# A zeroing memset in front of one row-tile load of a transformer block

## The chip, the cores and the metric

The kernel runs on one core of one Trainium2 chip. The metric is the device time of one execution in microseconds (us), as the median of several runs. The engines are named as the profile names them: PE is TensorE (matmuls), PEld its weight loads, DVE is VectorE, ACT is ScalarE, POOL is GpSimd, SP is SyncE, which here only issues DMAs. A name with a q behind it (SPq, ACTq) is an engine's instruction sequencer, which issues DMAs.

## The reference

The input x has 2048 rows of 1024 values, all in bfloat16. The kernel computes a transformer block: layer norm, sliding-window attention with a residual, a second layer norm, and a dense layer with SiLU, again with a residual.

```python
x = A_x
h  = x + attn(layernorm(x), A_wqkv, A_wo)       # 32 heads of 32, causal, window of 256 keys
h2 = h + silu(layernorm(h) @ B_w1) @ B_w2        # B_w1: 1024 x 3584, B_w2: 3584 x 1024
```

The layer norm subtracts the mean of a row and divides by the root of its variance plus 1e-5; it has no weights.

## The kernel before, in words

The 2048 rows are four blocks of 512, and a block is four row tiles of 128 rows, one row to a partition. The kernel goes through the blocks for Q, K and V (`v_group`, `qk_group`), with the attention of the block before woven in, then through the output projection (`wo_group`) and the two dense layers (`h1_group`, `mm2`). Everything is laid out by hand: big regions in SBUF (`r_w`, `r_a`, `r_o`, `r_t`, `r_e`, `r_n`) hold views that change their use over time, and the instructions of each engine run in the order in which the program issues them. Waits between engines follow from which views are read and written.

Only the start matters for the change. `x_ring` is a ring of eight row tiles of 1024 bfloat16 values a row, in `r_o`; `x_ring[0]` to `x_ring[3]` hold the four row tiles of block 0 (x0 to x3 below). `load_x` (L135) loads one tile by one DMA of 256 KB. `load_wqkv` (L141) loads 512 columns of the weights for Q, K and V, in one to four DMAs, with its queues taken in turn.

The program's first steps, in order:

1. On DVE, a memset of `warm` (a 128x128 tile of zeros, L144), and one of `eps` (one value a partition, L147). On ACT, a square root of `eps`, so that the table of functions is loaded (L149).
2. The loads: x0 on SP, x1 on ACT, the first 512 columns of the V weights in four quarters that go to SP and ACT in turn (each quarter has two of the eight 128-row pieces that a matmul group adds up), x2 on SP, the other 512 V columns in two halves on SP, x3 on SP, and 512 columns of the Q weights on SP.
3. On PE, nine matmuls on `warm` whose result nobody uses (`busy`, L167), which keep PE at work until data is there.

Then the layer norm of x0 and x1, in a form of its own, in which only the mean is taken off before the product and the scale is put on after it:

- `mean_first`: ACT sums the second half of x0 (L457), DVE takes the statistics of its first half (L174) and makes a mean of it (L459). ACT then sums x1 (L460). Each sum on ACT is an ACTIVATE and an ACTIVATION_READ_ACCUMULATOR.
- `center`: DVE takes the mean off x0 (L466) and off x1 (L468), in four quarters each, into `x_mid`.
- `turn_first`: PE transposes two 128x128 pieces into PSUM (L218), and ACT (for x0) or DVE (for x1) copies them into `lnT_b[0]` (L219), which is what the matmuls take as weights.
- The first group of real matmuls, `v_group(0, 0, 0)` (L240): eight matmuls of 512 columns, one for each 128-row piece of the V weights, with the other transposes between them. Ahead of it stand the first two pairs of transposes and two more matmuls on `warm` (`busy(2)`, L167).

After that the variances of x0 and x1 are taken on ACT (L485), x2 and x3 are normalised in the ordinary way on DVE (`ln_stats`, `ln_norm`), and tiles 3, 0 and 1 are transposed once more by DMA (`ln_transpose`, L206) for the Q and K matmuls.

The steps with which the order at the start is set:

```python
load_x(0, 0)
load_x(0, 1, nc.scalar)
load_wqkv(2 * D, 4, (nc.sync, nc.scalar))
load_x(0, 2)
load_wqkv(2 * D + 512, 2)
load_x(0, 3)
load_wqkv(0)
```

Of the kernel before, what the change touches and what calls it, by code (L numbers as in the profile page):

```python
# [44 lines left out]
def kernel(  # L45
# [10 lines left out]
    nc = tc.nc  # L56
# [38 lines left out]
    def view(region, off, *dims):  # L95
        n = 1
        for d in dims:
            n *= d
        ap = region[:, off:off + n]
        if len(dims) == 2:  # L100
            return ap.rearrange("p (a b) -> p a b", b=dims[1])
        if len(dims) == 3:
            return ap.rearrange("p (a b c) -> p a b c", b=dims[1], c=dims[2])
        return ap
# [5 lines left out]
    x_ring = [view(r_o, i * 1024, 1024) for i in range(8)]  # L110
# [23 lines left out]
    def load_x(b, j, queue=nc.sync):  # L134
        queue.dma_start(out=x_ring[(b % 2) * 4 + j], in_=x2d[(b * 4 + j) * P:(b * 4 + j + 1) * P, :])  # L135

    def load_wqkv(c0, parts=1, queues=(nc.sync,)):
        dst = wqk[:, :, c0:c0 + 512] if c0 < 2 * D else wv[:, :, c0 - 2 * D:c0 - 2 * D + 512]
        n = KT // parts
        for k in range(0, KT, n):  # L140
            queues[k // n % len(queues)].dma_start(out=dst[:, k:k + n, :], in_=wqkv_v[:, k:k + n, c0:c0 + 512])  # L141
# [7 lines left out]
    nc.scalar.activation(out=dummy[:], in_=eps[:], func=ACT.Sqrt)  # L149

    load_x(0, 0)
    load_x(0, 1, nc.scalar)
    load_wqkv(2 * D, 4, (nc.sync, nc.scalar))
    load_x(0, 2)
# [604 lines left out]
```

## Time and profile before

| | |
|---|---|
| median of 3 runs | 691.17 us (691.05 to 691.21) |
| span of the profiled execution, first to last instruction | 688.9 us |
| PE busy | 685.2 us, 99% of the span |
| DVE, ACT, POOL busy | 291.2, 244.2 and 160.8 us |
| mean granted TensorE clock | 1.000 |
| HBM read and written | 39.85 MB and 8.39 MB |

The profile is of one execution, whose span is 688.9 us; no other time of that execution is given, so its 688.9 stands against a median of 691.17, which also has what lies around the span. PE is busy for nearly all of it, but a busy PE is not yet PE at its peak, since matmuls are pipelined and their ends are modelled. All times in the views count from the first instruction of the span.

### The profile page before, as it was taken

To read this page: it belongs to the slowest core of one execution; us is meant where nothing else is said; L and a number is where in the kernel's file an instruction comes from. 1 tells how busy PE (TensorE), PEld (TensorE's weight loads), DVE (VectorE), ACT (ScalarE), POOL (GpSimd) and SP (SyncE) were. 2 spreads that over 40 slices of the span, in tenths; PEclk is the share of its full clock that TensorE was granted. 3 is DMA by queue.
4 is the path that set the end of the run, shared out by engine and by line. 5 is a ranking of instruction groups with operands and counts; after the bars stand their busy time and mean duration, and the time that the engine had idled before them with its cause. 6 is when DMAs were issued, how large, how long until landed. Compare 5 with 4: busy or idle time off the path is not lost.

```text
span 688.9 us, 14243 instructions
## 1 busy us (share of the span) xinstructions
PE 685.2 (99%) x6011; PEld 342.3 (50%) x6011; DVE 291.2 (42%) x613; ACT 244.2 (35%) x464; POOL 160.8 (23%) x295
## 2 busy tenths in 40 slices
PE   9999999999999999999999999999999999999998
PEld 4445555555555555544444444444444444444445
DVE  5267647744444449444316133342233251333111
ACT  7326666666667666421300033300133100233000
POOL 1006666566666656400000000000000000000000
PEclk9999999999999999999999999999999999999999
DMA  7832231126241889871023310022300123100110
GB/s 259 275 64 69 40 85 57 25 63 186 71 131 21 257 252 272 199 267 40 23 88 112 84 39 0 1 91 70 85 0 1 21 96 90 39 1 1 30 39 24
DMA packets 78641, 61.48 MB, mean 89 GB/s; under 512 B 52465, under 2 KB 62705, under 8 KB 78577
## 3 DMA queue, kind: packets, MB, share of 16 engines
q1 hardware_dynamic: 77888, 59.78, 30.2%
q8 instruction: 47, 0.77, 0.4%
q10 hardware_dynamic: 688, 0.79, 0.3%
q14 instruction: 18, 0.14, 0.1%
HBM read 39.85 MB, written 8.39 MB: 70 GB/s over the span
## 4 chain that ended last, share of the span: by engine, by line
PE 99%; DVE 0%; issue 0%
PE hacc L669 19%; PE hacc L706 18%; PE acc L250 17%; PE acc L706 11%; PE acc L669 9%; PE acc L240 7%; PE acc L271 7%; PE o_ps L383 5%; PE sc L303 3%; PE hacc L271 2%; PE sc L355 1%; PE o_ps L240 1%; PE o_ps L167 1%; PE sc L329 1%; PE acc L525 0%; PE o_ps L525 0%
## 5 line engine op out<-in xcount | busy, mean ns | idle before, releaser
L373 POOL TENSOR_SCALAR_AFFINE_SELECT r_e<-r_e 128x512 bf16<-128x512 bf16 (+1 forms) x288 | 157.8, 563 | 123.9 <-ACT r_e L363 60.8
L706 PEld LDWEIGHTS <-r_a 128*128 128x128 bf16 x952 | 90.9, 98 | 103.0
L669 PEld LDWEIGHTS <-r_w 128*128 128x128 bf16 x896 | 87.3, 98 | 104.8
L706 PE MATMUL hacc<-r_a 128*128 128x512 bf16 (+2 forms) x616 | 122.5, 360 | 0.0
L669 PE MATMUL hacc<-r_e,r_w 128*128 128x512 bf16 x456 | 100.9, 379 | 0.0
L315 ACT ACTIVATE r_e<-sc 128x768 bf16<-128x768 f32 x96 | 78.2, 814 | 47.9 <-PE sc L303 47.9
L678 ACT ACTIVATE r_n<-hacc 128x512 f32<-128x512 f32 x30 | 17.9, 597 | 178.9 <-PE hacc L669 178.9
L250 PEld LDWEIGHTS <-r_w 128*128 128x128 bf16 x512 | 47.1, 98 | 55.0 <-issue 1.0
L706 PE MATMUL acc<-r_a 128*128 128x512 bf16 x336 | 74.0, 379 | 0.0
L252 DVE CAST r_a<-acc 128x512 bf16<-128x512 f32 x56 | 38.7, 692 | 57.7 <-PE acc L250 57.4
L250 PE MATMUL acc<-r_t,r_w 128*128 128x512 bf16 x256 | 59.6, 380 | 0.0
L250 PE MATMUL acc<-r_w 128*128 128x512 bf16 x256 | 57.8, 380 | 0.0
L383 PEld LDWEIGHTS <-r_e 128*128 128x128 bf16 x1440 | 47.4, 96 | 17.9
L669 PE MATMUL acc<-r_e,r_w 128*128 128x512 bf16 x216 | 49.1, 379 | 0.0
L271 PE MATMUL acc<-r_o,r_a 128*128 128x512 bf16 x208 | 48.7, 380 | 0.0
L383 PE MATMUL o_ps<-r_a,r_e 128*128 128x33 bf16 x1440 | 48.1, 178 | 0.0
L721 DVE SCALAR_TENSOR_TENSOR r_t<-hacc,r_t 128x512 bf16<-128x512 f32 (+2 forms) x22 | 14.0, 635 | 56.7 <-PE hacc L706 56.7
L316 ACT ACTIVATE r_e<-sc 128x256 bf16<-128x256 f32 x96 | 37.6, 392 | 0.0
L271 PEld LDWEIGHTS <-r_a 128*128 128x128 bf16 x256 | 23.4, 98 | 26.9
L721 DVE SCALAR_TENSOR_TENSOR r_t<-acc,r_t 128x512 bf16<-128x512 f32 x12 | 8.3, 692 | 64.2 <-PE acc L706 64.2
L679 DVE SCALAR_TENSOR_TENSOR r_a<-r_n,hacc 128x512 bf16<-128x512 f32 x30 | 20.6, 687 | 33.0 <-ACT r_n L678 33.0
L669 PE MATMUL hacc<-r_a,r_w 128*128 128x512 bf16 x144 | 33.0, 379 | 0.0
(100 smaller groups left out, 539.6 us busy)
## 6 DMA issues: line engine op xcount, KB each, us to landing
r_w<-in_B_w_dram SPq DMA_DIRECT2D x8, 896.0 KB, 5.2
r_a<-in_B_w_dram SPq DMA_DIRECT2D x7, 1024.0 KB, 7.5
r_w<-in_A_wqkv_dram SPq DMA_DIRECT2D x4, 1024.0 KB, 7.8
h_dram<-r_t SPq DMA_DIRECT2D x16, 256.0 KB, 3.1
r_t<-h_dram SPq DMA_DIRECT2D x16, 256.0 KB, 2.8
out_dram<-r_t SPq DMA_DIRECT2D x31, 128.0 KB, 1.7
r_o<-in_A_x_dram SPq DMA_DIRECT2D x15, 256.0 KB, 4.6
r_e<-h_dram SPq DMA_DIRECT2D x3, 1024.0 KB, 5.7
```

The lines of the kernel that those rows point to most:

```text
L240: nc.tensor.matmul(acc, lhsT=lnT_b[b % 2][:, kt, j * P:(j + 1) * P], rhs=wv[:, kt, c * 512:(c + 1) * 512], start=(kt == 0), stop=(kt == KT ...
L250: nc.tensor.matmul(acc, lhsT=wqk[:, kt, col0:col0 + P], rhs=lnT_b[b % 2][:, kt, :], start=(kt == 0), stop=(kt == KT - 1))
L252: copy(out=(qT, kT)[which][b][:, g, :], in_=acc)
L271: nc.tensor.matmul(acc, lhsT=qT[b][:, g, j * P:(j + 1) * P], rhs=wo[:, g, c * 512:(c + 1) * 512], start=(g == 0), stop=(g == G - 1))
L303: nc.tensor.matmul(sc[hh // 2][half * 64:half * 64 + 64, hh % 2, col:col + qb - qa], lhsT=kT[t // 4][r0:r0 + DH, g, k0:k0 + 64], rhs=qT[b] ...
L315: nc.scalar.activation(out=tri[:, :, :, 64:256], in_=both, func=ACT.Exp, scale=scale)
L316: nc.scalar.activation(out=e[:, 1024:1280].rearrange("p (h q) -> p h q", q=P), in_=bank[:, :, 192:320], func=ACT.Exp, scale=scale)
L373: nc.gpsimd.affine_select(out=dst, in_=src, pattern=[[0, n] for n in dst.shape[1:-1]] + [[sgn, P]], compare_op=ALU.is_ge if upper else ALU ...
L383: nc.tensor.matmul(o_ps[pair][:, qt * 2 + hh, 0:VW], lhsT=chunk_of(i, bank, piece, pair, hh), rhs=v[:, b * 4 + kt, g * 4 + pair * 2 + hh, ...
L669: nc.tensor.matmul(acc, lhsT=w1[:, kt, ft * P:(ft + 1) * P], rhs=ln2T[b][:, kt, :], start=(kt == 0), stop=(kt == KT - 1))
L706: nc.tensor.matmul(acc[:, 0:c1 - c0], lhsT=gT[:, ft, j * P:(j + 1) * P], rhs=w2[ft // 4][:, ft % 4, c0:c1], start=(ft == 0), stop=(ft == F ...
L721: nc.vector.scalar_tensor_tensor(out=t_out[j % 2][:, c0:c1], in0=acc[:, 0:c1 - c0], scalar=0.5, in1=t_in[j % 2][:, c0:c1], op0=ALU.mult, o ...
```

## The change

The place in SBUF into which x1 is loaded is set to zero on VectorE before the load is issued. The load writes the same bytes, so it has to wait for the memset; the zeros are overwritten and never read. The load of x0, which is issued on SP ahead of it, is as before.

```diff
     load_x(0, 0)
+    nc.vector.memset(x_ring[1], 0.0)
     load_x(0, 1, nc.scalar)
     load_wqkv(2 * D, 4, (nc.sync, nc.scalar))
     load_x(0, 2)
```

## The prediction

> **What bounds the kernel now.** I read the page first, then the chain of waits, then the first nine microseconds row by row.
>
> The page (busy time and share of the span, then the shares of the chain that ended last) and two rows of the chain inside the first 9 us:
>
> ```profile
> PE 685.2 (99%) x6011; PEld 342.3 (50%) x6011; DVE 291.2 (42%) x613; ACT 244.2 (35%) x464; POOL 160.8 (23%) x295
> ...
> PE 99%; DVE 0%; issue 0%
> ...
> 1.05 4.02 PE o_ps L167 x9
> ...
> 8.72 1.73 PE o_ps L240 x8
> ```
>
> TensorE (PE) is the path from end to end: no slack swallows a delay of PE, and nothing off PE matters unless PE waits for it. The chain's two rows show a second thing: nine 512-column matmuls take 0.447 us each at the start, eight take 0.216 us each from 8.72. The timeline dates the doubling at about 6.2: the matmul at 5.88 is the last slow one, and two that begin at 6.37 take 0.59 together.
>
> So the change is judged at the first place where PE waits. The timeline there (start us, us, engine, line, operation):
>
> ```profile
> 0.81 0.40 SPq L135 DMA_DIRECT2D r_o<-in_A_x_dram  x1
> 0.89 0.11 DVE L144 MEMSET r_e<- 128x64 uint32 x1 [0.89 <-PEq L743]
> 0.95 0.06 DVE L147 MEMSET eps<- 128x1 f32 x1
> 1.06 0.39 ACTq L135 DMA_DIRECT2D r_o<-in_A_x_dram  x1
> 1.26 0.93 SPq L141 DMA_DIRECT2D r_w<-in_A_wqkv_dram  x2
> 1.49 0.97 ACTq L141 DMA_DIRECT2D r_w<-in_A_wqkv_dram  x2
> ...
> 4.30 1.06 ACT L460 ACTIVATE r_e<-r_o 128x1024 bf16<-128x1024 bf16 x1
> ...
> 5.26 0.19 ACT L460 ACTIVATION_READ_ACCUMULATOR r_e<-r_o 128x1 f32 x1
> 5.34 0.26 PEld L167 LDWEIGHTS <-r_e 128*128 128x128 bf16 x2
> 5.44 0.65 ACT L219 COPY r_w<-tp 128x256 bf16<-128x256 bf16 x2
> 5.45 0.63 PE L167 MATMUL o_ps<-r_e 128*128 128x256 bf16 x2
> ...
> 5.86 0.10 PEld L240 LDWEIGHTS <-r_w 128*128 128x128 bf16 x1 [0.26 <-ACT r_w L219]
> ```
>
> The second row tile (x1) is the DMA at 1.06. L460 sums it on ScalarE (ACT) at 4.30; behind L460 on the same engine stand the L219 copies of tile 0's transposes, and for the first copy the first real matmul (5.86) waits. At 5.44 the copy starts the moment L460's read of its sum ends: tile 0's weights-to-be wait for tile 1's sum.
>
> The DMA issues of those microseconds (last column: us from issue to landing):
>
> ```profile
> r_o<-in_A_x_dram SPq DMA_DIRECT2D x1, 256.0 KB, 2.7
> r_o<-in_A_x_dram ACTq DMA_DIRECT2D x1, 256.0 KB, 3.1
> r_w<-in_A_wqkv_dram SPq DMA_DIRECT2D x1, 256.0 KB, 3.7
> r_w<-in_A_wqkv_dram ACTq DMA_DIRECT2D x1, 256.0 KB, 4.3
> ```
>
> In order of issue they land at 3.5 (x0), 4.2 (x1), 5.0 (W0, first quarter of the V weights) and 5.8 (W1): some 0.7 to 0.8 us apart, in the order in which SP and ACT issued them, whichever queue it was. The two later quarters W2 (SP, 1.73) and W3 (ACT, 1.97) land at 6.9 and 7.9. Whoever is issued later loses a whole place in that line.
>
> **The change part by part.**
>
> *The memset.* One instruction on VectorE (DVE) behind eps, which ends at 1.01. Lower bound 0.06 us, the eps row (one word). The nearest row, the memset of 64 words in 112 ns against eps's 59, gives 0.84 ns a word. That row shows 128 bf16 zeros written as 64 words, so 1024 become 512 words: 0.059 + 511 x 0.84 ns = 0.49 us. Written as 1024 elements it would be 0.92, the upper bound. I take 0.49: it ends at about 1.50. The Trainium skill ("VectorE: DVE Perf Modes", "Zero memsets can be issued as uint32") has one cycle per word; at its 0.96 GHz that is an estimate of 0.53 us before the fixed part, and every issue below would be some 0.1 later. On DVE the next instruction waits for x0 until 3.55, so DVE itself loses nothing: 2.5 us of idle time hide the memset, and without that cover it would cost its 0.49.
>
> *The new wait.* It stands in ACT's queue in front of the x1 load. eps ended at 1.01 and the load was issued at 1.06, so 0.05 passes: issue at 1.55 instead of 1.06. Queued behind it on ACT are W1 and W3, both 0.49 later (1.98, 2.46). ACT's next computation needs x0, which lands at 3.5, so it loses nothing.
>
> *Where x1 now stands.* W0 (1.26) is ahead of it, W2 (1.73) behind. Lower bound: only the 0.49 is passed on, landing at 4.7. Value: it changes places with W0, landing at 5.0. Upper, behind W2 too: 5.8.
>
> *What follows.* L460 could start only when ACT was free (4.27), so x1 had 0.1 us to spare; it now starts at 5.0, 0.7 later. Its 1.06, the read and the copies move along, and the first matmul goes from 5.86 to 6.56. DVE's centring of tile 1 (L468), which waits for the same sum, moves by 0.7 too and is needed only after that matmul. PE idles from 5.88, where the two filler matmuls end, to 6.56.
>
> *What is given back.* W3 released the seventh matmul of the group at 7.9, some 0.12 late (it starts at 7.91, behind two transposes that begin at 7.68 and need 0.11); started later, PE no longer meets that wait if W3 lands by 8.3. The first matmul ran slowly until 6.2, losing 0.17; begun at 6.56 it would run fast, if the clock has risen by then. So +0.69 - 0.12 - 0.17 = **+0.40** if the rise comes at 6.2 as before. W3 now stands behind x2 (2.23) and beside the next 512 KB (2.74, landing at 9.1 before); if it lands at 8.9, PE loses 0.6 again: +1.0.
>
> *The clock.* Before the rise at 6.2, PE had been given work for 5.16 us from 1.05 on, with no gap longer than 0.14 us (between the last L167 of the nine and the first transpose). The change puts a gap of 0.69 us right there. Bounds: the rise is where it was (nothing lost), or the count starts again at 6.56 and takes 5.16 us. At half speed half of that is lost: 2.58. No row shows a rise over such a gap; I take the middle, 1.29, a rise at about 9.1. Sum: 0.69 - 0.12 - 0.17 + 1.29 = **+1.7**; ends +0.4 and +3.0. The Trainium skill ("TensorE: Matmul & The Clock Gate", "What's actually happening") speaks against the change here: full clock only after a busy window of about 3.4 us, on a grid that takes no notice of the kernel. By a full window after 6.56 the sum would be an estimate of +2.1; if 6.2 is a point of that grid, the next is 9.6 and it would be +1.9.
>
> Nothing later gives it back: the DVE steps from 9.0 to 14.6 that feed the transposes of tiles 3, 0 and 1 start from PE's last transposes and move with PE; behind 21 PE waits for nothing that counts, and its weights and the next tiles land before their use.
>
> The profiled execution has a span of 688.9; the median of the runs is 691.17, so 2.3 us lie around the span, which the change does not touch. I add the sum to the median: 691.17 + 1.7 = 692.9.
>
> **The rivals.**
>
> *A. The clock rises on time* (the other side: not slower by what can be told). Of the 5.16 us before the rise, 0.34 more become idle up to 6.2, about 7%; if that much is forgiven, only +0.4 to +1.0 remains: 691.6 to 692.2. For it: the rise already forgave 0.14. Against it: the gap is five times as long. It decides from the point where half the delay of the rise is under 1 us, a rise before about 8.5.
>
> *B. The wait is longer than I think.* If the memset takes 0.92 or more, x1 is issued at 1.98, behind W2; it lands at 5.8, L460 starts 1.5 late and the sum is 1.5 - 0.3 = +1.2 with the clock on time, +2.5 with the middle price for a late rise. Against it: the L144 row was packed into words.
>
> *C. The change does not do what it says.* A memset of 0.2 us or less leaves x1's issue at 1.26 or before, ahead of W0; it lands at 4.4 at most, 0.1 is to spare, and the end moves by 0.0 to 0.1. Against it: the slope of the two DVE rows.
>
> *D. Faster.* With x1 out of the way x0 may land 0.2 sooner, but the copies still stand behind x1's sum; a gain would need that sum sooner.
>
> **How the numbers follow.** Late rise with x1 in W0's place: 0.50, at +1.7 (1.4 to 3.0). A: 0.33. B: 0.10, nearly all on the slower side. C: 0.04. D: 0.03. About 0.2%, 1.4 us, is what a measurement of this kernel can tell from no change: slower 0.60, same 0.37, faster 0.03. The range takes in A from +0.4 and the late rise to +2.7: 691.5 to 693.9. The likeliest case alone has 692.5 to 694.1.
>
> **What would show it.** The x1 load issued at 1.5 to 1.6 and landed near 5.0; L460 at 5.0; first L240 weight load at 6.5 to 6.6; matmuls of 0.43 us spacing from there to about 9, where A would have 0.22. An x1 load that lands before 4.5, or an L460 at 4.3, proves me wrong; so does a first L240 that is late with fast matmuls behind it, and then A holds.

## The result and the profile after

The changed kernel takes 693.89 us (median of 6 runs, 692.75 to 695.72) against 691.11 before (six runs, with the three of the table among them), a ratio of 1.0037 with a 95% interval of 1.0027 to 1.0048: slower by 2.8 us, where 1.7 had been forecast. The profiled execution took 694.48, with a span of 692.7, which is 3.75 above the 688.9 of before. The line numbers of the changed kernel are one higher from L152 on: L461 is the sum of x1, L241 the first matmuls.

The same view of the first microseconds, after:

```profile
0.81 0.40 SPq L135 DMA_DIRECT2D r_o<-in_A_x_dram  x1
0.94 0.06 DVE L147 MEMSET eps<- 128x1 f32 x1
...
1.06 0.48 DVE L152 MEMSET r_o<- 128x512 uint32 x1
...
1.26 0.93 SPq L141 DMA_DIRECT2D r_w<-in_A_wqkv_dram  x2
...
1.58 0.46 ACTq L135 DMA_DIRECT2D r_o<-in_A_x_dram  x1
...
2.07 0.45 ACTq L141 DMA_DIRECT2D r_w<-in_A_wqkv_dram  x1
...
5.14 1.06 ACT L461 ACTIVATE r_e<-r_o 128x1024 bf16<-128x1024 bf16 x1 [0.79 <-DMA r_o<-in_A_x_dram]
...
6.60 0.10 PEld L241 LDWEIGHTS <-r_w 128*128 128x128 bf16 x1 [0.92 <-ACT r_w L220]
6.61 0.39 PE L241 MATMUL acc<-r_w 128*128 128x512 bf16 x1 [0.46 <-ACT r_w L220]
...
8.79 0.38 PE L241 MATMUL acc<-r_w 128*128 128x512 bf16 x1 [1.47 <-DMA r_w<-in_A_wqkv_dram]
...
14.04 1.03 PE L526 MATMUL o_ps<-r_w 128*128 128x512 bf16 x4
```

The matmuls of before that the rows of PE stand against:

```profile
5.88 0.55 PE L240 MATMUL acc<-r_w 128*128 128x512 bf16 x1
...
6.37 0.59 PE L240 MATMUL acc<-r_w 128*128 128x512 bf16 x2
...
10.29 1.03 PE L525 MATMUL o_ps<-r_w 128*128 128x512 bf16 x4
```

The first part is as foretold: a memset of 512 words, x1 issued at 1.58, its sum at 5.14, the first weight load at 6.60. The row at 8.79 is new. The third real matmul waits 1.47 us, not for ACT but for a DMA of weights: W1, which stands behind x1 in ACT's queue. The DMA issues of W0, x1 and W1, in this order (last column: us from issue to landing):

```profile
r_w<-in_A_wqkv_dram SPq DMA_DIRECT2D x1, 256.0 KB, 3.0
r_o<-in_A_x_dram ACTq DMA_DIRECT2D x1, 256.0 KB, 3.5
...
r_w<-in_A_wqkv_dram ACTq DMA_DIRECT2D x1, 256.0 KB, 6.7
```

W0 now lands at 4.3 and x1 at 5.1: they have changed places. W1, issued at 2.07, needs 6.7 us where it needed 4.3, and lands at 8.75. From 5.5 to 8.7 us both issuing queues move data, SP's (q1) and ACT's (q10, whose 0.79 MB in the whole run are its three loads); the columns are packets, MB and the share of the 16 DMA engines:

```profile
q1 hardware_dynamic: 477, 0.60, 57.0%
q10 hardware_dynamic: 450, 0.44, 41.7%
```

So W1 shares the engines with SP's loads, of which x2 (issued at 2.23) lands at 8.92, beside it. The chain that ended last says the same: that one transfer is now its first long piece.

```profile
PE 98%; DMA 1%; ACT 0%; DVE 0%; issue 0%
...
2.07 6.68 DMA r_w<-in_A_wqkv_dram
8.75 0.04 issue
8.79 0.38 PE acc L241
```

A third thing happens behind that wait. The windows below are cut where the trace's record of the clock has its steps (columns: stretch, its length, PE busy, then PEld, DVE, ACT, POOL, then granted clock, DMA share, GB/s):

```profile
5.98:9.40 3.42, 1.49 (x10) 0.69 (x10) 0.94 (x5) 1.30 (x6) 0.00 (x0) 1.00 1.03 349
9.40:12.81 3.41, 3.41 (x16) 1.78 (x15) 1.55 (x5) 3.04 (x7) 0.00 (x0) 0.50 1.08 390
12.81:692.60 679.79, 677.22 (x5975) 338.84 (x5973) 286.72 (x596) 236.71 (x448) 157.81 (x288) 1.00 0.31 85
```

The clock rose at 5.98, even earlier than before (6.21), behind 3.41 us of which PE had been busy for 3.39, and ahead of the new gap. But in the 3.42 us after it PE worked for only 1.49, and the next 3.41 ran at half clock.

Set against the same matmuls of before, PE is 0.73 late at the first real matmul, 2.20 at the third, and 3.76 from 12 us to the end. So the profiled 3.75 is, to rounding, 0.73 for the late x1, 1.47 for the late W1 and 1.56 for the fallen clock; nothing later adds or returns anything. Of the six runs three show a mean granted clock of 0.997 to 0.998 (694.48, 693.67 and 694.12 us), three show 1.000 (695.72, 693.22 and 692.75). One stretch of 3.41 us at half clock in 690 is a mean of 0.9975. So the third term is paid in some executions only: the two lowest runs, with a full record, are 1.6 and 2.1 us above before, near the 2.2 that the first two terms make. None of the 89 runs of before in the later comparisons shows less than 1.000. Why 695.72 came with a full record is not known, since only one execution has a trace; a first rise that came late could do it, for the record begins at the first rise.

### The profile page after: what moved, and what is told of

It reads as the page before. It is cut to its first block, busy times and chain, and to the rows that moved or that the text cites. A ratio compares the mean times of both kernels' runs of the same rounds, so it can differ in the third digit from the quotient of the medians.

```text
span 692.7 us, 14244 instructions
## 1 busy us (share of the span) xinstructions
PE 687.0 (99%) x6011; PEld 343.0 (50%) x6011; DVE 291.8 (42%) x614; ACT 244.1 (35%) x464; POOL 160.8 (23%) x295
## 4 chain that ended last, share of the span: by engine, by line
PE 98%; DMA 1%; ACT 0%; DVE 0%; issue 0%
PE hacc L670 19%; PE hacc L707 17%; PE acc L251 17%; PE acc L707 10%; PE acc L670 9%; PE acc L241 7%; PE acc L272 7%; PE o_ps L384 5%; PE sc L304 3%; PE hacc L272 1%; DMA r_w<-in_A_wqkv_dram 1%; PE sc L356 1%; PE o_ps L241 1%; PE sc L330 1%; PE acc L526 0%; PE o_ps L526 0%
```

## The experiments

Each kernel was timed beside the kernel before on the same chip; ratios are to that kernel, with 95% intervals. Theory 1 is that the wait costs through places that two loads lose in the order of issue, x1 and then W1, with the clock as a consequence.

**The memset alone.**

```diff
     load_x(0, 0)
+    nc.vector.memset(x_ring[5], 0.0)
     load_x(0, 1, nc.scalar)
```

> The same 512-word memset at the same point of VectorE's stream, but on the place of a tile of block 1 that is loaded at about 20 us, so that no early load waits for it. If the cost is the wait in front of ACT's loads (my theory): 691.1 us, within 0.2 of before, x1 issued at 1.06. If the memset itself costs (its 0.49 us on VectorE, or its writes beside the first DMAs): 692.5 or more, as in the changed kernel's 693.9.

Measured: 691.16 us, ratio 1.0000 (0.9991 to 1.0009). The memset itself costs nothing that the interval, some 0.6 us to either side, can tell; only what waits for it does.

**Only W1 waits.**

```diff
     load_x(0, 1, nc.scalar)
+    nc.vector.memset(wv[:, 2:4, 0:512], 0.0)
     load_wqkv(2 * D, 4, (nc.sync, nc.scalar))
```

> The memset (1024 bfloat16 values a partition, as in the change) is on the place of W1, the second quarter of the V weights, so that x1 is issued at 1.06 as before and only W1 and W3 wait, with issues at about 1.6 and 2.1. Theory 1 (what counts is how much stands in front of W1 when it is issued): W1 is still issued before W2 (1.73) and lands at about 5.8 to 6.3, in time for its matmul at 6.59: 691.1 to 691.6 us. Theory 2 (any half microsecond on W1 brings it beside x2 and it lands after 8): 692.5 to 694. Theory 3 (the late sum of x1 is the cause): 691.1, since x1 is on time.

Measured: 691.16 us, ratio 0.9999 (0.9990 to 1.0009). W1 was issued at 1.57 and landed at 6.15. The memset is as long as in the change, but x1's issue kept ACT's queue until 1.45 anyway, so W1 was moved by only 0.09, from 1.49 to 1.57, and that costs nothing. Theory 2's 692.5 to 694 is refuted for this kernel; what half a microsecond on W1 does while x1 is on time was not run. Theory 3 said the same number as theory 1, and the next pair decides there.

**Only x1 waits.** The base has all four quarters on SP; the second kernel adds the memset in front of x1.

```diff
+    nc.vector.memset(x_ring[1], 0.0)          # second kernel only
     load_x(0, 1, nc.scalar)
-    load_wqkv(2 * D, 4, (nc.sync, nc.scalar))
+    load_wqkv(2 * D, 4)
```

> No memset; all four quarters of the V weights on SP, so that ACT's queue has only x1. It is the base for the next kernel. The quarters are issued at about 1.26, 1.7, 2.2 and 2.7, in order and on one queue: W1 should land near 5.8, W3 near 7.6, before x2: 691.0 to 691.5 us.

> The kernel with all quarters on SP, and the change's memset in front of x1: x1 waits, no weight quarter stands behind it. Theory 1 (the weights behind the wait make most of the cost): x1 lands at 5.0, first real matmul at 6.6, no wait for W1, so 0.4 to 0.8 us above the kernel with all quarters on SP. Rival (the late x1 alone makes the cost, by the gap of 0.7 us and a clock that rises late or falls): 2 to 3 us above it.

Measured: 690.99 us, ratio 0.9997 (0.9987 to 1.0006), and 692.07 us, ratio 1.0016 (1.0004 to 1.0028). The late x1 alone costs 1.1 us. That is above theory 1's 0.4 to 0.8, which intervals of 0.7 and 0.8 us to either side do not exclude, and under the rival's 2 to 3. In its profile x1 is issued at 1.58, landed 3.5 later, and PE's longest wait in front of real work is the gap that was forecast. It is 0.95 us long here, because the clock had risen at 3.98 and the two filler matmuls ended sooner:

```profile
6.62 0.39 PE L241 MATMUL acc<-r_w 128*128 128x512 bf16 x1 [0.95 <-ACT r_w L220]
6.84 0.28 PE L219 MATMUL tp<-ident,r_e 128*128 128x128 bf16 x2
6.96 0.59 PE L241 MATMUL acc<-r_w 128*128 128x512 bf16 x2
```

The third matmul starts right behind the second, with no wait for W1 (on SP at 1.72, landed 6.8), at full clock. From the seventh matmul of the group on PE is 0.46 late against the kernel before, near the +0.40 that the prediction had for a late x1 with the clock on time. That profile is of a run of 691.30. Two of its ten runs had clocks of 0.997 and 0.998, and those were 694.38 and 694.53. The rest of the change's 2.8 us, some 1.7, needs W1 behind the wait; the intervals of the two ratios (1.0004 to 1.0028 and 1.0027 to 1.0048) just overlap, so the size of that part is rough.

**Another quarter behind the wait.**

```diff
+    nc.vector.memset(x_ring[1], 0.0)
     load_x(0, 1, nc.scalar)
-    load_wqkv(2 * D, 4, (nc.sync, nc.scalar))
+    load_wqkv(2 * D, 4, (nc.sync, nc.sync, nc.scalar, nc.scalar))
```

> The change, with the quarters of the V weights dealt out as SP, SP, ACT, ACT, so that W1 is issued on SP at about 1.73 (as W2 was) and W2 and W3 stand behind the wait on ACT. Theory 1 (x1's late sum costs 0.7, and beside x2 a quarter behind the wait lands 3 us later, which costs where that quarter is needed): W1 lands near 5.8, W2 at 8 to 9 with its matmul due at 7.7, so PE's wait moves from the third to the fifth matmul of the group and is shorter by 0.5: 692.9 to 693.6 us. Rival (the cost is x1 alone, and the wait for W1 is hidden in it): as with all quarters on SP, 692.0 to 692.3.

Measured: 692.82 us, ratio 1.0023 (1.0013 to 1.0034), 0.1 below the range of theory 1 and above the rival's; the interval, 692.1 to 693.5 us, takes in parts of both. W2, now in the place behind the wait (2.07), landed at 8.52, so the place did to W2 what it had done to W1. But the profiled run could not show the moved wait: x1 itself landed at 6.05 there, not 5.1, the first matmul came at 7.60, and W2 was in time. Three of the seven runs, this one among them, had a clock of 0.998 and took 693.63 to 693.94; the four at 1.000 took 692.01 to 692.82.

**A shorter memset.**

```diff
+    nc.vector.memset(x_ring[1][:, 0:128], 0.0)      # in the other kernel 0:512
     load_x(0, 1, nc.scalar)
```

> The change, with the memset cut to the first 128 values of x1's place (64 words, some 0.11 us): x1 is issued near 1.21, ahead of W0 (1.26), W1 near 1.65, ahead of W2 (1.73). Theory 1 (a place in the order of issue is lost or not): x1 lands by 4.4, L460 is late by at most 0.15: 691.1 to 691.4 us. Rival (the cost grows in proportion to the delay, 0.15 of 0.51): 691.9.

> The change, with the memset cut to the first 512 values of x1's place (256 words, some 0.27 us): x1 is issued near 1.38, behind W0, and W1 near 1.86, behind W2 but further ahead of x2 (2.23). Theory 1 (places): as the whole change, 693 to 694 us, with x1 landed at 5.0 and W1 after 7.5. Rival (proportion, 0.32 of 0.51): 692.8 and W1 landed near 7.

Measured: 691.52 us for 64 words, ratio 1.0002 (0.9993 to 1.0011), and 692.17 for 256, ratio 1.0016 (1.0007 to 1.0025). With 64 words x1 was issued at 1.10 and landed at 4.5; the 0.1 of theory 1's range that it missed by is not resolved, nor quite the rival's 691.9. With 256 words theory 1 missed by nearly 1 us: x1 was issued at 1.31, behind W0 (1.25), and landed at 5.2, as it said; but W1, at 1.75, landed at 7.3, before its matmul was due (7.8 in the profiled run), so that of the two loads x1 alone counted. The rival's W1 near 7 was right, its 692.8 too high. Places alone are too coarse. Over the traces in which x0 is issued ahead of x1 the weight load behind x1 in ACT's queue was issued at 1.49 to 1.50 and landed at 5.75 to 6.28; at 1.57 to 1.58, landed at 6.15 to 6.28; at 1.75, landed at 7.3; at 2.07, landed at 8.2 to 8.75. That is some 4 to 5 us of landing for each us of issue. Landing at 7.3 and later it comes within 0.3 us of SP's x2 (7.4 to 8.9), with which it shared the engines in the changed kernel. The 256-word profile also shows what the forecast had put into the changed kernel, a clock that has not risen when the first real matmul starts:

```profile
5.40 0.63 PE L168 MATMUL o_ps<-r_e 128*128 128x256 bf16 x2
6.77 0.61 PE L241 MATMUL acc<-r_w 128*128 128x512 bf16 x1 [0.74 <-ACT r_w L220]
7.17 0.42 PE L219 MATMUL tp<-ident,r_e 128*128 128x128 bf16 x2
7.38 1.06 PE L241 MATMUL acc<-r_w 128*128 128x512 bf16 x2
...
10.66 0.38 PE L241 MATMUL acc<-r_w 128*128 128x512 bf16 x1
```

The matmuls from 6.77 on are at half clock until 10.51; PE was 0.89 late at the first of them and 2.43 late at the end of the group.

**Gaps filled.** The first kernel adds eight matmuls on zeros, two of 256 columns and six of 512, into the two gaps of the change; the second only four of 512 into the wait for W1.

```diff
 ...
     for i in range(2):                       # first kernel: range(4)
         busy(2)
 ...
+    def filled(kt):
+        if kt == 2:
+            for i in range(6):               # second kernel: range(4)
+                busy(4)
+        steps_0(kt)                          # the transposes, as before
 ...
```

> The change, with eight more matmuls on zeros whose result is not used: two of 256 columns ahead of the first real matmul (TensorE then works until 6.3 instead of 5.95), and six of 512 columns ahead of the third, where TensorE waits for W1 (1.3 us at full clock). They fit into the waits, so they take no time at full clock. Theory 1 with the clock as a part of the cost (gaps make the clock rise late or fall again in some runs): 692.5 to 693.2 us, and single runs within 1 us of each other. Rival (the clock is no part of it, only the arrival of x1 and W1): 693.9 as the change, or more by what does not fit.

> The change, with four more matmuls of 512 columns on zeros ahead of the third real one, where TensorE waits for W1: 0.86 us of work in a wait of 1.47. Theory 1 (gaps let the clock fall or rise late): fewer runs with a second slow stretch, median 692.9 to 693.4 us, if no fetch of instructions lands in the transposes; about 694.6 if it does. Rival (the clock is no part): 693.9.

Measured: 694.82 us, ratio 1.0050 (1.0036 to 1.0064), and 694.00, ratio 1.0050 (1.0025 to 1.0075). Neither is the gain that theory 1 forecast. In the first the clock did stay up (risen at 3.88, and all five runs at 1.000, 694.1 to 695.2). Two of its rows, the third real matmul, and the matmul that stands at 10.29 before and at 14.04 in the changed kernel:

```profile
8.60 0.38 PE L241 MATMUL acc<-r_w 128*128 128x512 bf16 x1
...
12.42 1.03 PE L534 MATMUL o_ps<-r_w 128*128 128x512 bf16 x4
```

PE was 2.01 late at the third matmul and 2.14 at 12.42; the changed kernel was 2.20 and 3.76 late at the same two places. So of the 1.56 that the changed kernel lost in between the filled one lost 0.13; the rest is the fall of the clock. Then the filled kernel lost 1.67 at 19 us, waiting for the DMA transposes. In the second kernel the five runs part by the clock: 692.60, 692.65 and 694.00 at 1.000, 695.75 at 0.998, 696.84 at 0.995. Four matmuls were not enough to hold it in two of the five.

**Where the 1.67 us went.** The kernel before with eight matmuls of 128 columns added at the same point:

```diff
 ...
+    def filled(kt):
+        if kt == 2:
+            for i in range(8):
+                busy(1)
+        steps_0(kt)
 ...
```

> No memset; the kernel before with eight more matmuls of 128 columns ahead of the third real matmul, as many more instructions as in the kernel that filled the change's gaps, but only 8 x 0.054 = 0.43 us of work. If the 1.7 us which that kernel lost at 19 us come from a fetch of instructions that its longer program moved into the DMA transposes: 692.5 to 693.3 us, with the fetch at 16 to 18 us. If they come from something else: 691.4 to 691.7, with the first fetch near 24.

Measured: 692.53 us, ratio 1.0016 (1.0007 to 1.0025), as forecast if the fetch of instructions is the cause. The DMA view of 15.5 to 20 us there (queues, then the issue of the transposes):

```profile
q8 instruction: 1, 0.02, 2.2%
...
r_w<-r_o SPq DMA_TRANSPOSE x3, 4.3
```

and of the kernel before, from 14.6 to 17.6:

```profile
q1 hardware_dynamic: 1318, 0.33, 48.4%
...
r_w<-r_o SPq DMA_TRANSPOSE x3, 2.8
```

One packet of 16 KB of instructions, begun at 16.46 and 1.60 us long, lies among the transposes, which take 4.3 instead of 2.8; PE waits for them (the first line in the waits of 14 to 24 us that concerns PE's matmuls):

```profile
PE o_ps L240 <- DMA r_w<-r_o: 1.5, 1, 1.5
```

Before, the first such packet comes at 24.5, in the changed kernel at 28.7, in the kernel with four matmuls at 26.3, in all three clear of the transposes. In the kernel with the gaps filled it came at 17.8.

**The opposite of the change.** ACT's loads go ahead of its square root.

```diff
-    nc.scalar.activation(out=dummy[:], in_=eps[:], func=ACT.Sqrt)
     load_x(0, 0)
     load_x(0, 1, nc.scalar)
     load_wqkv(2 * D, 4, (nc.sync, nc.scalar))
+    nc.scalar.activation(out=dummy[:], in_=eps[:], func=ACT.Sqrt)
```

> No memset; the kernel before with ACT's three loads ahead of its square root of eps, so that x1 is issued near 0.8 instead of 1.06, W1 near 1.2 and W3 near 1.7: the change's opposite. Theory 1 (x1 had 0.1 us to spare and the copies behind it were due at 5.42 anyway; W3 was 0.12 late): 690.9 to 691.2 us. Rival (the end follows x1's issue in proportion, some 5 us for each us, as 2.78 for 0.51): 689.8. If x1 is issued ahead of x0, x0's own sum is late by 0.7 and the time is 691.5 to 692.

Measured: 693.24 us, ratio 1.0025 (1.0014 to 1.0035): slower, and by more than the 692 of the third case. Issued together with x0 at 0.80, x1 landed at 4.67 and x0 at 4.50; in the other traces x0, always issued at 0.80, landed at 3.4 to 4.2. The first matmul came 0.87 late, and here too a packet of instructions (19.07, 1.65 us) fell on a transpose, for another 1.25. Two of its eight runs had a clock of 0.998, at 693.33 and 693.46, within the range of the six at 1.000 (691.35 to 693.74).

**Wider filler.** On the kernel with all quarters on SP and the memset in front of x1:

```diff
     for i in range(2):
-        busy(2)
+        busy(4)
```

> The kernel with all quarters on SP and the change's memset in front of x1 (692.07 us, two of ten runs at 694.4 and 694.5 with a granted clock of 0.997 and 0.998), with one edit: the two matmuls on zeros ahead of the first real one have 512 columns instead of 256, so that at half clock TensorE works until about 6.3 instead of 5.9 and the gap before the first real matmul is 0.3 instead of 0.7. No instruction is added. Theory 1 (part of the cost is the clock that rises late or falls after the gap): 691.5 to 691.8, and no run with a clock under 1. Rival (the gap itself is all of the cost): 692.0 to 692.4, and the two kinds of runs as before.

Measured: 693.28 us, ratio 1.0031 (1.0017 to 1.0045). Both sides missed. Six of twelve runs kept a clock of 1.000 and lie at 692.05 to 692.78, five at 0.998 lie at 693.78 to 695.58, one at 0.995 took 696.70. In the profiled one the clock had risen at 4.36, so the wider filler ran at full clock and ended as early as the narrow one does at half clock; x1 landed at 6.07, which left a gap of 1.58 us; and the fall followed:

```profile
4.36:7.77 3.41, 1.55 (x9) 1.00 1.03 331
7.77:11.18 3.41, 3.41 (x15) 0.50 1.08 385
```

(PE alone: stretch, length, busy, granted clock.) The runs are parted by their clock, 692.26 at 1.000 against 694.61 at 0.998 (medians). Not all of that is the clock's: in the profiled run PE was 1.75 late at the first matmul, by the landing of x1, and lost 1.39 more by the clock. What the runs refute is that a filler of that size prevents the fall.

Why x1 lands at 5.1 in most profiles with the full wait and at 6.05 to 6.07 in two of them is open. A load reports its landing in sixteen parts; in those two the last trails the ninth by over 1 us, in the others by 0.2 to 0.3. No run tells what held it. Nor was the kernel run in which W1 alone is issued at 2.07, with x1 on time, so the price of the late W1 rests on the wait of 1.47 us in the changed kernel's trace and on the difference to the pair with x1 alone.

## Why the prediction was right, and where it was not

The direction and the range held. The way to them did not in its likeliest case: the trace shows what the prediction had named as a sign against itself, a first matmul that is late with fast matmuls behind it.

1. The memset, its packing into 512 words and its price held: 0.485 us against 0.49, issue at 1.58 against 1.55.
2. x1 in W0's place held: landed 5.06 against 5.0, first weight load 6.60 against 6.56, PE 0.73 late against 0.69.
3. The step that failed is "Queued behind it on ACT are W1 and W3". Both were dated, but only W3's landing was priced, with +1.0 as the sum if it lands at 8.9. W1 got no price at all. It was due at 7.2, landed at 8.75 and cost 1.47; 1.7 us of the median are its share by the pair with x1 alone. By the prediction's 0.7 to 0.8 us a place W1, fifth in order, would have landed at an estimated 6.6, in time. That spacing did not hold for it: from 5.5 on it shared the engines with SP's loads. W3, which had a price, landed at 10.07 and cost nothing, since the seventh matmul, at 10.54, was later still.
4. "The clock" was priced at 1.29 as a late rise and measured 1.56 in the profiled run, but as a fall. The rise came on time, as rival A had it, and A's conclusion of +0.4 to +1.0 failed all the same, because of step 3 and of the fall. The late rise that was forecast exists (the 256-word kernel, risen at 10.51), but the changed kernel's trace does not show it. The gap of 0.14 us that the prediction names ahead of the rise is idle time in no row: PE is busy for all of 4.87 to 5.01. The Trainium skill ("TensorE: Matmul & The Clock Gate", "What's actually happening") has the clock follow windows of 3.4 us on a grid of its own. The traces agree: in the changed kernel the steps are at 5.98, 9.40 and 12.81, 3.41 apart, and in all thirteen traces that hold a record of the clock the steps are whole multiples of 3.413 us apart. The same section has the return to half clock after an idle window; here 1.49 us of work in 3.42 did not prevent it.
5. The things given back were small and real. The first matmul ran at full clock (0.39 against 0.55 us). The 0.12 of W3 can't be told apart in the changed kernel, whose clock had fallen by then; in the kernel with x1 alone both show, with PE 0.74 late at the first matmul, 0.58 at the second and 0.46 at the seventh.

So 1.7 held the direction and 0.6 of the size, and it is partly luck that it did: a term of 1.5 us was missing, and the term for the clock, right in size for another reason, is paid by only some executions. The range, up to 693.9, took the measured 693.89 in by 0.01.

## What to carry to other kernels

When a wait is put into a queue, give each DMA behind it a landing time and a due time, not only the one that the wait is meant for; here the load that waited cost 1.1 us by itself, and with the one behind it the cost was 2.8. A gap of TensorE in the first ten microseconds is paid twice in those executions whose clock falls or rises late for it. Instructions added to fill a gap are not free: they moved the fetch of code into the DMA transposes here, and that cost 1.7 us, about what the fallen clock cost (1.6).

## What was not expected of the hardware

- Clock: of the windows cut at the clock's steps, those with PE busy for 1.33, 1.49 and 1.55 of 3.41 us were followed by half clock, and those with 1.91 to 2.5 were not (1.91 at 18.5 us, in the kernel with eight matmuls of 128 columns). For the rise, 2.63 and 2.68 of 3.41 were not enough (256-word kernel), 2.83 was (gaps filled). In these traces the fall so lies between 1.55 and 1.91 and the rise between 2.68 and 2.83, and a filler has to be sized by both.
- One packet of instructions of 16 KB, 1.60 to 1.69 us long, lay beside the DMA transposes in three kernels, and PE lost 1.25 to 1.9 us there; in the other eleven traces no such packet fell among them, and they took 2.7 to 2.9 us each.
- Two row tiles issued within 0.01 us of each other landed within 0.2 us of each other; x0 came at 4.50, where it came at 3.4 to 4.2 when it was issued first.
